# The indirect stores of routing records written through views of their table that are declared disjoint

## The chip, the cores and the metric

The kernel runs on one core of a Trainium2 chip. The metric is the device time of one execution in microseconds (us). TensorE (PE) does matmuls, VectorE (DVE) and ScalarE (ACT) do elementwise work, GpSimd (POOL) does reductions across partitions and issues indirect DMAs, SyncE (SP) issues the other DMAs. Each engine works through its own instructions in a fixed order and waits at an instruction until the semaphores that it names have come.

## The reference

Three layers follow one another on 2304 tokens of width 512. The third sends each token to one of eight experts; where a token's place in its expert's list is kept is what this change is about.

```python
# 1 attention: 4 batches x 8 heads, 576 tokens, head size 64, 128 random features
q_p, k_p = phi(q * scale), phi(k * scale)   # phi: exp(x @ omega.T - |x|^2/2 - max over features)
x = (q_p @ (k_p.T @ v)) / (q_p @ sum(k_p) + 1e-6)
# 2 dense layer, 512 -> 2048 -> 512
h = x @ w_in
x = (h * clip(h + 3, 0, 6) / 6) @ w_out
# 3 mixture of 8 experts, 512 -> 1024 -> 512; tokens with x @ w_skip <= 0 pass unchanged
e = argmax(x @ w_gate); g = softmax(x @ w_gate)[e]
out = x + g * (relu(x @ w1[e]) @ w2[e])
```

## The kernel before

The tokens go through the dense layer in six chunks of 512, 256, 384, 384, 384 and 384 (`CHS`), numbered 0 to 5. For each chunk sixteen steps run over the hidden width in pieces of 128. A step is a first product (L615, twelve matmuls: the operands are split into a high and a low part, and three products of the parts are summed; the last four use the low part `wil`, which SP loads again for every step into one of two buffers, L601), its activation on ACT and DVE (L621 to L636), and a second product into one bank of PSUM for each block of 128 tokens (L646).

Attention for batches 0 and 1 runs ahead of chunk 0 and within it; attention for batches 2 and 3 is spread among the steps of chunks 1 to 3. For a pair of heads (b, p) it projects queries on PE (L430), copies them on ACT to two tiles `pr` (L458), takes the maximum over the 128 features on POOL (`q_max`, a partition_all_reduce, L466), subtracts it on DVE (`q_sub`, L471), takes the exponential on ACT (`q_exp`, L475), and multiplies by the key sums on PE (`x_num`, L485, 40 small matmuls). The result is divided, transposed (L508) and written to `xh` and `xl`, the inputs of the dense layer.

When a chunk is done, its output is sent to DRAM (`x1d`), and the routing of its tokens follows: scores (`gate_dot`), the expert and the rank within it (`route_max` to `route_copy`), and the slot in the table (`route_slot`, L714 to L736). Then `route_put` (L738) stores, for each block of 128 tokens, 128 records of eight bytes (token number and weight) with an indirect DMA of POOL into the table `tab` in DRAM, at the slots. A chunk has as many stores as it has blocks: 4, 2, 3, 3, 3, 3, together 18. The slots of different tokens differ, but all 18 stores name the same rows of `tab` as their output, so the framework, which keeps the order of writes to overlapping regions, lets each store wait for the landing of the one before it.

The table is read in two places that this text speaks of. During chunk 5, SP loads 576 records of the fullest expert (`ga_rec`, L869) and 64 more of another (`s_rec`, `take_rec2`, L821); with these POOL gathers rows of `x1d` (L810) for the expert's matmuls, and at the end scatters the results to `out` (L815, L838). What is left goes through a loop at the end (L1482), whose body is not entered with these inputs.

The order on each engine comes from a list planner (`Schedule`): every operation is added with an engine, a cost, a due time and what it reads and writes, `plan` simulates them, and the instructions are emitted in that order. The planner knows the stores as POOL work of 1.04 us each, due at the chunk's routing time; it doesn't know of the waits between them, which the framework adds afterwards. DMAs that POOL issues signal their landing on one of eight counters, `DMASW0` to `DMASW7`, taken in turn.

Of the kernel before, what the change touches and what calls it, by code (L numbers as in the profile page):

```python
# [24 lines left out]
NT, DM, DFF = 2304, 512, 2048  # L25
# [4 lines left out]
C0 = [sum(CHS[:c]) for c in range(NCH + 1)]  # L30
# [11 lines left out]
TABN = NE * SEG  # L42
# [155 lines left out]
def performer_moe_kernel(  # L198
# [27 lines left out]


    tab = dram.tile([TABN + 128, 2], I32, name="tab")
    x1d = dram.tile([NT, DM], F32, name="x1d")
    wils = dram.tile([FT, 128, DM], F32, name="wils")  # L230

# [436 lines left out]
    rt = {}  # L668
# [68 lines left out]

    def route_put(c, t):  # L738
        G.indirect_dma_start(  # L739
            out=tab[0:TABN, :], out_offset=bass.IndirectOffsetOnAxis(ap=rt["slot"][:, t:t + 1], axis=0),  # L740
            in_=rt["rec"][:, t], in_offset=None, bounds_check=TABN - 1, oob_is_err=False)

    def begun(n8, name):
# [587 lines left out]
    def after(c):  # L1331
        t = START[c + 1]
        for k in range(TPC[c]):
            i = C0[c] // 128 + k
            sc.add("ACT", act(DM), t - 6, lambda k=k, i=i: x1_copy(i, accs[c, k]), r=[("acc", c, k), "x1p"], w=[("x1", i)],
                   t=[("ps", ("acc", c, k)), ("x1", i)])
            sc.add("SP", 2 * SPC, t + 1, lambda i=i: x1_out(i), r=[("x1", i)], o=[("wil", (c + 1, 3 + 2 * k))], w=[("x1d", c)], t=[("x1", i)],
                   nbytes=128 * DM * 8)
            for e in range(NE + 1):
                sc.add("DVE", 0.7, t + (AT["dot"] if c != CA - 1 else 0) + k * 9 if c < NCH - 1 else t + AT["dot5"] + k, lambda i=i, e=e: gate_dot(i, e), r=[("x1", i), "wg"], w=[("lg", c)],  # L1340
                       t=[("x1", i)])
        u = t + AT["route5"] if c == NCH - 1 else t + 25 if c == CA - 1 else t + AT["route"]
        sc.add("DVE", 0.3, u, lambda: route_max(c), r=[("lg", c), "rt"], w=[("rt0", c), "rt"])
        sc.add("ACT", 0.2, u, lambda: route_exp(c), r=[("rt0", c)], w=[("rt1", c)])
        sc.add("DVE", 0.9, u, lambda: route_hot(c), r=[("rt1", c)], w=[("rt2", c)])
        sc.add("PE", 0.1, u, lambda: route_rank(c), r=[("rt2", c)], w=[("rt3", c)], t=[("ps", ("rank", c))])
        sc.add("DVE", 0.2, u, lambda: route_copy(c), r=[("rt3", c)], w=[("rt5", c)], t=[("ps", ("rank", c))])
        sc.add("DVE", 3.1, u, lambda: route_slot(c), r=[("rt5", c), "cnt"], w=[("rt4", c), "cnt"])
        for k in range(TPC[c]):

            sc.add("POOL", 1.04, u, lambda k=k: route_put(c, k), r=[("rt4", c), "tab0"], w=["rt", ("tab", c)], nbytes=1024,
                   o=["ga_rec", "s_rec"] if c >= CA else [])
# [185 lines left out]
```

## Time and profile before

| | |
|---|---|
| time, median of 3 runs | 624.19 us (622.95 to 625.39) |
| the profiled execution: its own time | 624.3 us |
| its span in the trace | 622.4 us |
| mean granted clock of TensorE | 0.991 of full |
| PE busy | 599.8 us, 96% of the span |
| DVE busy | 440.7 us, 71% |
| ACT busy | 291.1 us, 47% |
| POOL busy | 110.3 us, 18% |

Times in the trace are in us from the start of the span. The execution's own time is 1.9 us longer than the span. The chain of waits that ended last holds only the last scatter and does not reach back into the kernel, so for this profile the waits of TensorE, which is busy nearly throughout, say more.

### The profile page before, as it was taken

The numbers are of one execution on the slowest core, as the hardware profiler recorded it, in microseconds if no ns is written. First come the engines' busy times: TensorE is split into PE (matmuls) and PEld (weight loads), VectorE is DVE, ScalarE is ACT, GpSimd is POOL, SyncE is SP. The second block draws the span as 40 slices with busy tenths as digits, with TensorE's granted clock in tenths as the row PEclk, the third lists the DMA queues.
The fourth block names the chain that finished last, engine by engine and source line by source line (L and its number), as shares of the span: only waits on it lengthen the run. The fifth ranks groups of instructions, "written<-read, shape, count | busy, mean of one in ns | idle before, by whom it ended". The sixth has DMA issues, their size and how long they took to land. (4 is left out here: it accounts for less than half of the span.)

```text
span 622.4 us, 11811 instructions
## 1 busy us (share of the span) xinstructions
PE 599.8 (96%) x4350; PEld 510.6 (82%) x4350; DVE 440.7 (71%) x1198; ACT 291.1 (47%) x672; POOL 110.3 (18%) x83
## 2 busy tenths in 40 slices
PE   9899999999999999999999999799999999999994
PEld 8677777788888898889988888799899889797883
DVE  3889999998769969863269673549722887449861
ACT  4776988677532456442234653332222323443220
POOL 2225034000020022221002043100010002402431
PEclk9999999999999999999999999899999999999998
DMA  7566466366366346322334313124212423892311
GB/s 281 163 196 189 151 202 212 117 217 203 99 231 185 99 141 176 90 67 56 68 91 148 108 65 52 34 85 136 68 52 68 135 89 99 265 351 69 92 45 53
DMA packets 38412, 81.66 MB, mean 131 GB/s; under 512 B 5740, under 2 KB 6380, under 8 KB 38352
## 3 DMA queue, kind: packets, MB, share of 16 engines
q1 hardware_dynamic: 36144, 76.90, 40.1%
q0 software_dynamic: 1776, 3.56, 1.9%
q8 instruction: 35, 0.57, 0.4%
q10 hardware_dynamic: 432, 0.43, 0.2%
q14 instruction: 25, 0.20, 0.1%
HBM read 65.88 MB, written 15.25 MB: 130 GB/s over the span
## 5 line engine op out<-in xcount | busy, mean ns | idle before, releaser
L646 PE MATMUL acc<-wo,gh 128*128 128x512 f32 x576 | 184.2, 401 | 0.2 <-ACT gh L630 0.2
L661 DVE CUSTOM_DVE_ANT_0 idle<-x,wg 128x512 uint8<-128x512 f32 x162 | 115.2, 711 | 7.6 <-ACT x L652 4.5
L646 PEld LDWEIGHTS acc<-wo,gh 128*128 128x128 f32 x576 | 103.9, 188 | 20.0 <-ACT gh L630 0.8
L621 ACT ACTIVATE g<-mm,half_t 128x384 f32<-128x384 f32 (+2 forms) x96 | 55.8, 581 | 126.6 <-PE mm L615 118.9
L646 PE MATMUL acc<-wo,gl 128*128 128x512 f32 x288 | 114.4, 397 | 0.1
L466 POOL PARTITION_ALL_REDUCE mx<-pr x32 | 67.6, 2160 | 234.1 <-ACT pr L458 227.7
L626 DVE SCALAR_TENSOR_TENSOR g<-g,mm 128x384 f32<-128x384 f32 (+2 forms) x96 | 52.8, 551 | 66.1 <-ACT g L621 65.6
L615 PE MATMUL mm<-xh,wih 128*128 128x384 f32 (+2 forms) x384 | 85.3, 344 | 0.1
L630 ACT CAST gh<-g 128x384 fp32r<-128x384 f32 (+2 forms) x96 | 49.3, 514 | 73.4 <-PE acc L646 46.6
L615 PE MATMUL mm<-xl,wih 128*128 128x384 f32 (+2 forms) x384 | 82.5, 336 | 0.0
L636 DVE TENSOR_TENSOR gl<-g,gh 128x384 fp32r<-128x384 f32 (+2 forms) x96 | 53.3, 556 | 33.4 <-ACT gh L630 33.2
L615 PEld LDWEIGHTS mm<-xh,wih 128*128 128x128 f32 x384 | 67.8, 189 | 9.0 <-DVE xl L520 0.2
L615 PEld LDWEIGHTS mm<-xl,wih 128*128 128x128 f32 x384 | 66.7, 188 | 2.8
L615 PE MATMUL mm<-xh,wil 128*128 128x384 f32 (+1 forms) x320 | 66.0, 328 | 1.0 <-DMA wil<-wils 1.0
L646 PEld LDWEIGHTS acc<-wo,gl 128*128 128x128 f32 x288 | 54.1, 188 | 13.8 <-DVE gl L636 0.9
L739 POOL DMA_INDIRECT tab<-rec,r_sloti x18 | 18.4, 1024 | 211.4 <-DVE rec L735 177.3
L615 PEld LDWEIGHTS mm<-xh,wil 128*128 128x128 f32 x320 | 54.6, 188 | 1.3 <-DMA wil<-wils 1.3
L393 ACT ACTIVATE kp<-att,kmx 128x128 f32<-128x128 f32 x160 | 45.5, 384 | 14.9 <-DVE kmx L378 14.8
L471 DVE TENSOR_TENSOR pr<-pr,mx 128x576 f32<-128x576 f32 x32 | 31.3, 978 | 8.4 <-POOL mx L466 8.4
L378 DVE TENSOR_REDUCE kmx<-att 128x2 f32<-128x256 f32 (+1 forms) x64 | 28.1, 482 | 8.2 <-PE att L372 5.1
L475 ACT ACTIVATE pr<-pr 128x576 f32<-128x576 f32 x32 | 22.1, 690 | 22.3 <-DVE pr L471 21.6
L485 PE MATMUL att<-kv,pr 128*64 128x65 f32 x640 | 25.1, 234 | 4.8 <-ACT pr L475 4.2
(204 smaller groups left out, 768.2 us busy)
## 6 DMA issues: line engine op xcount, KB each, us to landing
wil<-wils SPq DMA_DIRECT2D x80, 256.0 KB
w<-w_in SPq DMA_DIRECT2D x16, 512.0 KB
w<-w_out SPq DMA_DIRECT2D x16, 512.0 KB
vx<-vn SPq DMA_DIRECT2D x16, 322.5 KB
qr<-qt SPq DMA_DIRECT2D x16, 288.0 KB
out<-x SPq DMA_DIRECT2D x18, 256.0 KB
x1d<-x SPq DMA_DIRECT2D x18, 256.0 KB
kr<-kt SPq DMA_DIRECT2D x15, 288.0 KB
```

The costliest lines, as they stand in the source:

```text
L378: V.reduce_max(out=mx[:, 0:n], in_=st[key, b, p, g, h][:, 0:n * M].rearrange("p (g m) -> p g m", m=M), axis=AX.X, negate=True)
L393: A.activation(kp[:, i], ps[:, i * M:(i + 1) * M], AF.Exp, bias=mx[:, i:i + 1], scale=1.0)
L466: G.partition_all_reduce(mx, st["e", b, p, r], channels=128, reduce_op=bass_isa.ReduceOp.max)
L471: V.tensor_sub(pr, pr, st.pop(("qm", b, p, r)))
L485: T.matmul(ps[m:m + 64, i * 130 + r * 65:i * 130 + r * 65 + 65], st["e", b, p, r][:, s0 + m:s0 + m + 64], kv[:, r * 65:(r + 1) * 65], star ...
L615: T.matmul(ps[:, 0:CHS[c]], w[:, k, :], x[:, k, d], start=(n == 0), stop=(n == 3 * KC - 1))
L621: A.activation(t, mmp[c, f][:, 0:CHS[c]], AF.Relu, bias=half_t, scale=2.0 ** -UP / 6.0)
L626: V.scalar_tensor_tensor(out=t, in0=t, scalar=1.0, in1=mmp.pop((c, f))[:, 0:CHS[c]], op0=ALU.min, op1=ALU.mult)
L630: A.copy(gh, gt[c, f])
L636: V.tensor_sub(gl, t, gh.bitcast(F32))
L646: T.matmul(accs[c, t], g[:, ts], w[:, r, f % 2, :], start=(f == 0 and j == 0), stop=(f == FT - 1 and j == 2))
L661: V.tensor_tensor_reduce(out=idle.bitcast(mybir.dt.uint8), in0=x1[i], in1=wg[:, e, :], scale=1.0, scalar=0.0, op0=ALU.mult, op1=ALU.add, a ...
```

## The change

The table gets 18 views, one for each block of tokens, that the framework is told are disjoint, and each store writes through the view of its block. The reads of the table still name the table itself. The rest of the kernel is as it was; two more lines ahead of them move the numbers of all later lines by two.

```diff
--- before.py
+++ after.py
@@ -226,6 +226,8 @@
 
 
     tab = dram.tile([TABN + 128, 2], I32, name="tab")
+
+    tabs = dram_disjoint_views(tab, NT // 128)
     x1d = dram.tile([NT, DM], F32, name="x1d")
     wils = dram.tile([FT, 128, DM], F32, name="wils")
 
@@ -737,7 +739,7 @@
 
     def route_put(c, t):
         G.indirect_dma_start(
-            out=tab[0:TABN, :], out_offset=bass.IndirectOffsetOnAxis(ap=rt["slot"][:, t:t + 1], axis=0),
+            out=tabs[C0[c] // 128 + t][0:TABN, :], out_offset=bass.IndirectOffsetOnAxis(ap=rt["slot"][:, t:t + 1], axis=0),
             in_=rt["rec"][:, t], in_offset=None, bounds_check=TABN - 1, oob_is_err=False)
 
     def begun(n8, name):
```

No instruction changes its place on any engine: only the waits differ. On POOL, the place during chunk 3 at which the three stores of chunk 2 stand, with the last `q_max` pairs of attention around them (`mx` is the maximum, `rec` and `r_sloti` the records and slots) and the first store of chunk 3 behind; before:

```order
L466 ISA mx<-pr 128x576 [waits DVE_49,Activation_49] x4
L739 DMA tab<-rec,r_sloti 19456x2 [waits DMASW5_49,DVE_49]
L739 DMA tab<-rec,r_sloti 19456x2 [waits DMASW6_49,DVE_49]
L739 DMA tab<-rec,r_sloti 19456x2 [waits DMASW7_49,DVE_49]
L466 ISA mx<-pr 128x576 [waits Activation_49,Pool_49] x2
L739 DMA tab<-rec,r_sloti 19456x2 [waits DMASW0_49,DVE_49]
```

and with the change (`DMASW0` in the third store is the counter whose turn has come again, last used by the very first store of the kernel):

```order
L468 ISA mx<-pr 128x576 [waits DVE_49,Activation_49] x4
L741 DMA tab<-rec,r_sloti 19456x2 [waits DVE_49] x2
L741 DMA tab<-rec,r_sloti 19456x2 [waits DMASW0_49,DVE_49]
L468 ISA mx<-pr 128x576 [waits Activation_49,Pool_49] x2
L741 DMA tab<-rec,r_sloti 19456x2 [waits DMASW1_49,DVE_49]
```

The stores of one chunk no longer name the landing of the store before them, and the instructions behind them are the same. On SP, the place in chunk 5 where the records of the fullest expert are loaded; before:

```order
L870 TENSOR_LOAD ra [waits DVE_49]
L870 ISA x2
L873 ISA
L873 DMA ga_rec<-tab 128x2x2 [waits DMASW6_49]
L873 ISA
L873 DMA ga_rec<-tab 128x2x2
L874 ISA
L874 DMA ga_rec<-tab 64x2
```

and with the change:

```order
L872 TENSOR_LOAD ra [waits DVE_49]
L872 ISA x2
L875 ISA
L875 DMA ga_rec<-tab 128x2x2 [waits DMASW4_49,DMASW5_49,DMASW3_49,DMASW6_49,DMASW2_49,DMASW7_49,DMASW1_49,DMASW0_49]
L875 ISA
L875 DMA ga_rec<-tab 128x2x2
L876 ISA
L876 DMA ga_rec<-tab 64x2
```

The first load of the records, which before named only the counter of the last store, now names all eight counters; what stands behind it on SP is unmoved.

## Rows read from the trace of the kernel before

**Rows 1.** The page, part 1: busy time, share of the span and instructions of each engine

```profile
PE 599.8 (96%) x4350; PEld 510.6 (82%) x4350; DVE 440.7 (71%) x1198; ACT 291.1 (47%) x672; POOL 110.3 (18%) x83
```

**Rows 2.** Waits of TensorE, 210 to 622: who waited for whom, total, times, longest

```profile
PE att L485 <- ACT pr L475: 4.0, 2, 3.2
PE mm L615 <- DMA wil<-wils: 1.0, 1, 1.0
```

**Rows 3.** TensorE timeline, 370 to 402: start, duration, engine, line, operation [idle before <-releaser]

```profile
375.75 1.34 PE L485 MATMUL att<-kv,pr 128*64 128x65 f32 x40
376.91 0.64 PE L409 MATMUL att<-vx,kp 128*64 128x65 f32 x16
...
387.95 0.40 PE L646 MATMUL acc<-wo,gl 128*128 128x512 f32 x1
...
392.70 2.22 PE L485 MATMUL att<-kv,pr 128*64 128x65 f32 x36 [0.80 <-ACT pr L475]
394.85 1.36 PE L615 MATMUL mm<-xh,wih 128*128 128x384 f32 x4
396.05 0.88 PE L615 MATMUL mm<-xl,wih 128*128 128x384 f32 x4
396.76 0.87 PE L615 MATMUL mm<-xh,wil 128*128 128x384 f32 x4
```

**Rows 4.** Windows: stretch, length, busy (x instructions) PE PEld DVE ACT POOL, clock, DMA, GB/s

```profile
392.70:396.10 3.40, 3.40 (x41) 3.28 (x42) 2.21 (x8) 0.93 (x2) 0.00 (x0) 0.55 0.00 0
580.00:613.50 33.50, 33.50 (x188) 28.45 (x186) 21.22 (x79) 10.09 (x23) 13.19 (x14) 1.00 0.24 71
```

**Rows 5.** GpSimd timeline, 370 to 402

```profile
376.62 1.01 POOL L739 DMA_INDIRECT tab<-rec,r_sloti  x1 [5.66 <-DVE rec L735]
380.81 0.97 POOL L739 DMA_INDIRECT tab<-rec,r_sloti  x1 [3.18 <-DVE xl L520]
386.07 0.97 POOL L739 DMA_INDIRECT tab<-rec,r_sloti  x1 [4.28 <-DMA tab<-rec,r_sloti]
387.06 3.88 POOL L466 PARTITION_ALL_REDUCE mx<-pr  x2
```

**Rows 6.** VectorE timeline, 370 to 402

```profile
380.25 0.82 DVE L520 TENSOR_TENSOR xl<-att,xh 128x384 fp32r<-128x384 f32 x2 [0.97 <-ACT xh L516]
389.03 1.71 DVE L471 TENSOR_TENSOR pr<-pr,mx 128x576 f32<-128x576 f32 x1 [7.96 <-POOL mx L466]
```

**Rows 7.** ScalarE timeline, 370 to 402

```profile
378.32 1.34 ACT L458 COPY pr<-att 128x288 f32<-128x288 f32 x4
...
391.96 0.68 ACT L475 ACTIVATE pr<-pr 128x576 f32<-128x576 f32 x1
```

**Rows 8.** GpSimd timeline, 500 to 600

```profile
515.61 0.97 POOL L739 DMA_INDIRECT tab<-rec,r_sloti  x1 [58.54 <-DVE rec L735]
...
523.25 0.97 POOL L739 DMA_INDIRECT tab<-rec,r_sloti  x1 [3.80 <-DMA wraw<-w]
...
594.70 1.05 POOL L810 DMA_INDIRECT xgc<-x1d,ga_rec  x1 [0.27 <-POOL xgc L809]
```

**Rows 9.** SyncE waits, 500 to 560

```profile
SPq L873 <- DMA tab<-rec,r_sloti: 3.3, 1, 3.3
```

**Rows 10.** SyncE timeline, 515 to 540

```profile
529.79 0.53 SPq L601 DMA_DIRECT2D wil<-wils  x1
```

**Rows 11.** TensorE timeline, 525 to 536

```profile
531.99 0.86 PE L615 MATMUL mm<-xl,wih 128*128 128x384 f32 x4
533.88 0.97 PE L615 MATMUL mm<-xh,wil 128*128 128x384 f32 x4 [1.03 <-DMA wil<-wils]
```

**Rows 12.** One line's instructions, L739: durations in ns min/median/max, first and last start

```profile
L739 POOL DMA_INDIRECT tab<-rec,r_sloti x18: 967/974/1483, 220.2 to 592.9; - x18
L739 POOLq EVENT_SEMAPHORE  x17: 17/17/3092, 223.2 to 589.1; - x17
...
DMA to landing us min/median/max: 2.1/2.9/5.6
```

## The prediction

> **What bounds the kernel now.** I began with the busy shares on the page: TensorE (PE) is busy for 599.8 us, 96% of the span, and the next engine, VectorE (DVE), for 71% [rows 1]. The reader is to see that a gain elsewhere counts only where PE stands still for it or runs slower for it. So the second view was the waits of PE from 210 us on, since the first routing store comes at 220.2 [rows 12]. The rows shown are the only two of more than half a microsecond there: 4.0 us, in two pieces, for the exponentials of attention (`pr`, L475), and 1.0 us for a low weight part (`wil`) [rows 2]. Third, the timelines around these two places, followed backwards from engine to engine until something is found that the change touches. Both end at an indirect store of routing records, and the two are worked out below as places A and B. Last, the tail: from 580.00 to 613.50 PE is busy for 33.50 of 33.50 us at full clock [rows 4], so whatever PE gains before 580 arrives at the end, and nothing that merely comes earlier on another engine there does.
>
> **The change, part by part.** Nothing is added to any engine and nothing moves; a store takes POOL 967 to 1483 ns before and after [rows 12]. What goes is the wait of a store for the landing of the one before it, 2.1 to 5.6 us from issue to landing [rows 12]. A store in the change still waits for a counter that a DMA eight turns back used, which landed long ago, or for nothing but its records. Which of the 18 stores matter is decided by what is queued behind them on POOL.
>
> *Place A, the three stores of chunk 2.* They start at 376.62, 380.81 and 386.07, and at 387.06 the last pair of `q_max` follows without a gap [rows 5]. That the pair starts 0.02 us after the last store's instruction, over 2 us before that store can have landed, shows that POOL itself is free as soon as the instruction is over. The inputs of the pair, four copies of ACT, were ready at 378.32 + 1.34 = 379.66 [rows 7]. So the pair stood 7.4 us behind stores that were waiting for each other. DVE, done at 381.07, stood idle for 7.96 us until the first maximum came, and took it at 389.03 [rows 6]; the second exponential was over on ACT at 391.96 + 0.68 = 392.64 [rows 7], and PE went on with `x_num` at 392.70 [rows 3]. PE had finished its work ahead of that at 387.95 + 0.40 = 388.35 [rows 3].
>
> In the change the stores come one behind the other: 376.62 + 1.01 + 0.97 + 0.97 = 379.57 [rows 5]. The pair then starts at 379.7, when its inputs are there. From the start of the pair to the end of the last exponential it took 392.64 - 387.06 = 5.58 us, so that `x_num` could start at 385.3, three microseconds before PE comes to it. Were all three stores as long as the longest, 1.48 us, POOL would be free at 381.1 and `x_num` ready at 386.7, still ahead of PE. The wait therefore vanishes, with 1.7 to 3 us to spare.
>
> The price of the wait is more than its 4.0 us. After it, from 392.70 to 396.10, the granted clock was 0.55 [rows 4], so mostly the lower of the two levels, 1.2 GHz, where it was 2.4 GHz before. `x_num` undisturbed took 376.91 - 375.75 = 1.16 us for 40 matmuls, and four matmuls of the first product at full clock 396.76 - 396.05 = 0.71 us [rows 3]. So without the wait the second group of that step (L615, `xl`) starts at 388.35 + 1.16 + 0.71 = 390.22 instead of 396.05 [rows 3]: **5.8 us**, of which 4.0 are the waits, 3.35 - (0.9 x 1.16 + 0.71) = 1.6 the lower clock, and 0.2 the four matmuls between the two waits. The low end, if the clock fell for another reason, is 4.0. I take 5.8, since PE did nothing else unusual ahead of the fall.
>
> Here a rule speaks against the change. The rows say that a store took POOL at most 1.48 us, whatever DVE did beside it [rows 12]; the stores brought forward to 377.6 and 378.6 now stand beside a DVE that works until 381.07 [rows 6]. The Trainium skill (SBUF — State Buffer, section "SBUF: two separate sides") holds that GpSimd cannot write the descriptors of its own DMAs while DVE uses their shared port in a fast mode, and the next section of that page has a DMA of about 620 ns take about 3100 ns in this way. By that figure, an estimate, the two stores would hold POOL until 383.8 and `x_num` would be ready at 389.4, one microsecond late, which would leave 618.2 us. The traces so far don't bear it out: in none of the 18 stores does the instruction reach half of that.
>
> *Place B, the three stores of chunk 4.* They start at 515.61 and, waiting for each other, up to 523.25 [rows 8]; the last had landed at about 523.25 + 2.1 = 525.35, and SP stood for 3.3 us until then at the load of the expert's records (`ga_rec`) [rows 9]. Queued behind it on SP are the other loads of records and the load of the next `wil`, which went out at 529.79 [rows 10]. PE needed it one group after 531.99, so at 531.99 + 0.71 = 532.70, and got it at 533.88 [rows 11]: **1.2 us**. In the change the third store starts at 515.61 + 2 x 0.97 = 517.55. SP's wait ends with the landing of the last of the three: with the median landing, 2.9 us [rows 12], at 520.5, before SP comes to it (525.35 - 3.3 = 522.05); with the longest, 5.6, at 523.2. SP so gains 2.2 to 3.3 us, more than the 1.2 that are needed. That SP now names eight counters instead of one costs seven semaphore instructions that are already satisfied; on POOL such a one takes 17 ns [rows 12], so some 0.1 us, inside that reserve. The gathers of `x1d` and their transposes, which wait for the same records, come earlier by the same amount, so they don't take the place of the wait.
>
> *The other twelve stores.* Behind those of chunks 0, 1 and 3 POOL has nothing whose input is ready, and no wait of PE in [rows 2] leads there: nothing. Behind those of chunk 5 stands the last gather at 594.70 [rows 8], which feeds only the last weighing of results, after the last matmuls, and PE is busy without a gap until 613.50 [rows 4]: nothing as long as PE sets the end, and should PE shrink there too, the gather comes earlier with the stores.
>
> *Sum.* 624.3 us of the profiled execution - 5.8 - 1.2 = 617.3. It lies 0.1 above the median of the runs, 624.19, so I write 617.2.
>
> **The rivals.**
> - *Only A pays.* Three stores in flight at once could land later than one by one, and then SP waits as before. Condition: a landing after 522.05 + (3.3 - 1.2) = 524.15, so 6.6 us after the third store's start, where 5.6 was the longest seen. For it: three at once have not been seen here on this table. Time: 624.2 - 5.8 = 618.4.
> - *A new wait at A.* Between the pair of maxima and `x_num` ACT and DVE have pieces of the dense layer's steps to do, which lay in the pause before; if one of them, waiting for PE in its turn, now stands ahead of an exponential, half of the gain may go: 624.2 - 2.9 - 1.2 = 620.1. Against it: a reserve of 1.7 to 3 us.
> - *Nothing changes.* POOL could be held by the store in flight, inside the instruction rather than ahead of it, as the descriptors of the next store have to wait for room. Then every store is as late as before: 624.2. Against it: POOL began other work 0.02 us after a store [rows 5], though not another store.
> - *Slower.* One mechanism at B: if the small writes of stores in flight hinder each other on the way to DRAM, the last lands late, SP stands at the records with `wil` behind it, and PE stands for `wil`. PE goes on 533.88 - 525.35 = 8.5 us after the landing. Compared with before, PE loses what the landing loses against 525.35, so the gain of A is used up if the last store lands after 525.35 + 5.8 = 531.2, that is 13.6 us after its start. Three times the longest landing, 16.8 us, would give 534.35: 624.2 - 5.8 + 9.0 = 627.4. For it speaks only that landings differ by more than a factor of two already one by one; against it, that 13.6 is 2.4 times the longest.
>
> **How the numbers follow.** Forecast 0.74; only A 0.10; a new wait at A 0.05; nothing 0.07; slower 0.04. The forecast's own range is that of the runs of before, 1.2 either way: 616.0 to 618.4. To hold 8 in 10 it must take in the case in which only A pays, with its own spread, and part of the next: 615.6 to 620.4. A change of under 0.5%, 3.1 us, can't be told from none. Faster by more (below 621.1): the first three cases, 0.89, of which I give 0.01 to their spread, 0.88. Within: 0.08. Slower: 0.04.
>
> **What would show it.** Right at A: three stores on POOL within about 3 us of the first, the `q_max` pair some 7 us earlier in relation to them, DVE's idle time of 8 us ahead of `q_sub` gone, no wait of PE at L485, and the granted clock at full behind it. Right at B: the load of `ga_rec` without a wait of 3 us on SP, and no wait of PE for `wil`. In all else the busy times stay, and the tail after 580 is the same, some 7 us earlier. Wrong would be: gaps of 2 us and more between stores of one chunk as before, store instructions of 2 us and more, or a later landing that SP waits for.

## The result: 615.1 us, and the profile after

The change takes 615.07 us (median of 6 runs, 614.49 to 615.74); the kernel before took 623.25 us (6 runs, 622.25 to 625.39; three of them are those of the first table, and the three others have the median 622.72). The ratio is 0.987, with an interval of 0.9853 to 0.9888: faster by 1.1 to 1.5%. The forecast was 617.2 with a range of 615.6 to 620.4, so the time lies 0.5 us below the range. The profiled execution of the change has a span of 612.6 us, against 622.4.

Both predicted waits are gone. The page of the change, part 1, against [rows 1], and then the waits of TensorE from 210 to 622 (who waited for whom, total, times, longest), against [rows 2]:

```profile
PE 595.7 (97%) x4350; PEld 507.4 (83%) x4350; DVE 440.7 (72%) x1198; ACT 291.2 (48%) x672; POOL 110.7 (18%) x83
```

```profile
PE att L374 <- DVE g L628: 0.2, 1, 0.2
```

The same instructions run, PE is busy 4.1 us less for the same 4350 matmuls, and the two rows on L485 and on `wil` are missing. What is left is a fifth of a microsecond.

Place A. GpSimd's timeline (start, duration, engine, line, operation [idle before <-releaser]), which answers to [rows 5]:

```profile
373.92 1.01 POOL L741 DMA_INDIRECT tab<-rec,r_sloti  x1 [5.65 <-DVE rec L737]
375.24 0.97 POOL L741 DMA_INDIRECT tab<-rec,r_sloti  x1 [0.30 <-issue]
376.51 0.97 POOL L741 DMA_INDIRECT tab<-rec,r_sloti  x1 [0.30 <-issue]
377.51 3.88 POOL L468 PARTITION_ALL_REDUCE mx<-pr  x2
```

The three stores follow each other at 1.3 us, where they took 4.2 and 5.3 us before, and the pair of maxima begins 3.59 us after the first store instead of 10.44. VectorE's, ScalarE's and TensorE's timelines answer to [rows 6], [rows 7] and [rows 3]:

```profile
379.48 1.71 DVE L473 TENSOR_TENSOR pr<-pr,mx 128x576 f32<-128x576 f32 x1 [1.33 <-POOL mx L468]
```

```profile
382.41 0.69 ACT L477 ACTIVATE pr<-pr 128x576 f32<-128x576 f32 x1
```

```profile
385.24 0.40 PE L648 MATMUL acc<-wo,gl 128*128 128x512 f32 x1
385.56 1.39 PE L487 MATMUL att<-kv,pr 128*64 128x65 f32 x40
386.88 0.96 PE L617 MATMUL mm<-xh,wih 128*128 128x384 f32 x4
387.68 0.86 PE L617 MATMUL mm<-xl,wih 128*128 128x384 f32 x4
```

The second exponential is over at 383.10, 2.5 us before PE comes to `x_num`, and the row of `x_num` has no wait. The granted clock behind it, from the windows (columns as in [rows 4], whose first row it answers to), is full:

```profile
385.50:389.00 3.50, 3.50 (x53) 3.37 (x53) 2.26 (x9) 0.45 (x1) 0.00 (x0) 1.00 0.02 8
```

From the first store of chunk 2 to the group `xl` behind `x_num` it was 396.05 - 376.62 = 19.43 us, and is 387.68 - 373.92 = 13.76: place A gave 5.67 us, where 5.8 were forecast.

Place B. The timelines of GpSimd, SyncE and TensorE, which answer to [rows 8], [rows 9, 10] and [rows 11]:

```profile
507.18 0.97 POOL L741 DMA_INDIRECT tab<-rec,r_sloti  x1 [64.12 <-DVE rec L737]
508.46 0.97 POOL L741 DMA_INDIRECT tab<-rec,r_sloti  x1 [0.30 <-DVE a_oh L1127]
509.74 1.08 POOL L741 DMA_INDIRECT tab<-rec,r_sloti  x1 [0.30 <-DVE used L1133]
```

```profile
513.90 0.97 SPq L875 DMA_DIRECT2D ga_rec<-tab  x2
...
518.32 0.53 SPq L603 DMA_DIRECT2D wil<-wils  x1
```

```profile
523.57 0.86 PE L617 MATMUL mm<-xl,wih 128*128 128x384 f32 x4
524.27 0.87 PE L617 MATMUL mm<-xh,wil 128*128 128x384 f32 x4
```

SP's load of the records no longer waits, `wil` goes out 11.14 us after the first store of the chunk instead of 14.18, and the matmul on it comes at once, 17.09 us after that store instead of 18.27: place B gave 1.18, where 1.2 were forecast. One store still costs what it did, and lands as it did, against [rows 12] (durations in ns min/median/max, first and last start):

```profile
L741 POOL DMA_INDIRECT tab<-rec,r_sloti x18: 971/977/1484, 217.5 to 579.2; - x18
...
DMA to landing us min/median/max: 2.1/3.0/5.0
```

The two spans differ by 9.8 us, though, and A and B together by 6.85. Of the rest 2.70 us lie ahead of the first store of chunk 2, and, with 220.17 us against 217.47 for the very first store, in a part of the program in which the change touches nothing. The windows of the head tell the executions apart; from 28 to 36 us, first before, then the change:

```profile
28.00:36.00 8.00, 7.79 (x106) 6.55 (x104) 5.68 (x16) 5.96 (x18) 0.86 (x1) 0.79 0.61 209
```

```profile
28.00:36.00 8.00, 7.79 (x107) 6.57 (x105) 6.84 (x19) 6.79 (x20) 2.46 (x2) 1.00 0.89 283
```

The execution of before had a stretch of lower clock there, that of the change had one from 20 to 24 us, and others have none in the head. Both kernels have executions with either kind of head, as the table below shows, and this pair of profiles so overstates the change.

### The profile page after: what moved, and what is told of

The parts are those of the page before. It is cut to its first block, busy times and chain, and to the rows that moved or that the text cites. A ratio compares the mean times of both kernels' runs of the same rounds, so it can differ in the third digit from the quotient of the medians.

```text
span 612.6 us, 11813 instructions
## 1 busy us (share of the span) xinstructions
PE 595.7 (97%) x4350; PEld 507.4 (83%) x4350; DVE 440.7 (72%) x1198; ACT 291.2 (48%) x672; POOL 110.7 (18%) x83
## 5 line engine op out<-in xcount | busy, mean ns | idle before, releaser
L374 PE MATMUL att<-wb,kr 64*128 64x128 f32 x320 | 26.5, 292 | 1.3 <-DVE xl L522 0.8
```

Source lines behind the costliest of these rows:

```text
L374: T.matmul(st[key, b, p, g, h][:, i * M:(i + 1) * M], x[half(h), min(c * 128, S - 128):min(c * 128 + 128, S)], wb[half(h), :], start=True, ...
```

## The experiments

Twelve runs followed, on three further chips, four to a chip, each time beside the kernel before. "A" and "B" are the places of the prediction. The time at each is read from GpSimd's timeline, from the first store of chunk 0 to that of chunk 3 (place A lies between) and from there to that of chunk 5 (place B). Where no wait of PE is left between, they are 222.0 and 136.6 us in every trace, within 0.05, so what stands above these is what the place costs in that execution (in the row "the wait filled", A holds the added matmuls too):

| kernel, as traced | first store of chunk 0 | of 3 | of 5 | 0 to 3 | 3 to 5 | A | B |
|---|---|---|---|---|---|---|---|
| before | 220.17 | 447.91 | 585.83 | 227.74 | 137.92 | 5.7 | 1.3 |
| views unused | 218.41 | 446.24 | 583.81 | 227.83 | 137.57 | 5.8 | 1.0 |
| views for chunk 2 | 217.91 | 444.30 | 582.28 | 226.39 | 137.98 | 4.4 | 1.4 |
| views for chunk 4 | 218.54 | 446.41 | 583.00 | 227.87 | 136.59 | 5.9 | 0.0 |
| views for the others | 220.02 | 449.98 | 589.18 | 229.96 | 139.20 | 8.0 | 2.6 |
| the wait filled | 218.21 | 445.96 | 586.89 | 227.75 | 140.93 | 5.8 | 4.3 |
| third store waits | 218.44 | 441.99 | 578.62 | 223.55 | 136.63 | 1.6 | 0.0 |
| maxima first, no views | 220.04 | 442.08 | 579.71 | 222.04 | 137.63 | 0.0 | 1.0 |
| the change, first chip | 217.47 | 439.50 | 576.10 | 222.03 | 136.60 | 0.0 | 0.0 |
| the change, second chip | 218.32 | 444.62 | 581.22 | 226.30 | 136.60 | 4.3 | 0.0 |
| the change, third chip | 218.78 | 445.29 | 581.93 | 226.51 | 136.64 | 4.5 | 0.0 |
| the change, fourth chip | 220.17 | 442.17 | 578.77 | 222.00 | 136.60 | 0.0 | 0.0 |
| change and maxima first, third chip | 217.63 | 439.58 | 576.21 | 221.95 | 136.63 | 0.0 | 0.0 |
| change and maxima first, fourth chip | 218.01 | 440.01 | 576.62 | 222.00 | 136.61 | 0.0 | 0.0 |

### The second chip: parts of the change, and the change again

Before on this chip: 622.58 us.

**Views declared, and not used.**

```diff
     tab = dram.tile([TABN + 128, 2], I32, name="tab")
+
+    tabs = dram_disjoint_views(tab, NT // 128)
```

> The views are declared and no store uses them: the instructions and their waits are those of the kernel before. Theory T (places A and B are all that the change does, 5.7 + 1.3 us; what the medians differ by beyond that, 8.2 - 7.0 = 1.2 us, is the spread of executions in the first 60 us): 0.0 us against before, within 0.5. Rival H (the change also does something to the start of the program): if the declaration alone did it, -1.2 us.

Measured: 622.87 us, ratio 0.9998 (0.9983 to 1.0014). PE waits 4.0 us at L487, as in [rows 2]. The declaration alone does nothing that shows.

**Views for the stores of chunk 2 alone.** The declaration is as above; the diffs of this and the next partial versions show the store alone, with the rest of its line left out (`...`).

```diff
-            out=tab[0:TABN, :], ...
+            out=(tabs[C0[c] // 128 + t] if c in (2,) else tab)[0:TABN, :], ...
```

> Only the three stores of chunk 2 use the views; the other fifteen name the table as before and wait for one another. Theory T: place A alone, -5.7 us (617.5 where before has 623.2), PE's wait of 4.0 us at the exponentials gone, its wait of 1.0 us for wil still there. Rival H: A and B together are larger than their traces show, so -6.5 to -6.9. Rival, B causes part of A: less than -5.

Measured: 621.96 us, ratio 0.9982 (0.9966 to 0.9997). That is 0.6 us less than before, where 5.7 were expected: a miss, far below the 5.8 us of place A, though its wait is gone. By its number alone this is the rival "B causes part of A" of the expectation; TensorE's waits show that something else stands in the place of A:

```profile
PE att L432 <- ACT kv L417: 2.4, 1, 2.4
PE mm L617 <- DMA wil<-wils: 1.1, 1, 1.1
```

A new wait of 2.4 us at `q_proj` (L432), for a copy of ScalarE. I call it the hold, and come back to it.

**Views for the stores of chunk 4 alone.** The diff is that of chunk 2 with `c in (4,)`.

> Only the three stores of chunk 4 use the views. Theory T: place B alone, -1.3 us, PE's wait for wil gone, its 4.0 us at the exponentials still there with the low clock behind. Rival H: -2 or more.

Measured: 621.36 us, ratio 0.9975 (0.9959 to 0.9992), 1.2 us less than before. PE's wait for `wil` is gone and the 4.0 us at L487 stand. Place B alone has its forecast worth.

**The change again.**

> The change itself once more, beside before on the same chip. Theory T: -7.0 us, so that the 8.2 us of the first medians shrink; of that 5.7 at A and 1.3 at B. Rival H: -8.2 again.

Measured: 619.49 us, ratio 0.9936 (0.9914 to 0.9958), so only 3.1 us less than before; on the first chip it was 8.2. Both theories of the expectation (7.0 and 8.2) were missed. The trace has the hold. TensorE's timeline, its windows and ScalarE's timeline of this run:

```profile
375.02 0.64 PE L411 MATMUL att<-vx,kp 128*64 128x65 f32 x16
375.58 1.39 PE L432 MATMUL att<-qr,wb 64*128 64x288 f32 x6
379.35 0.75 PE L432 MATMUL att<-qr,wb 64*128 64x288 f32 x2 [2.38 <-ACT kv L417]
```

```profile
381.00:384.40 3.40, 3.40 (x12) 3.40 (x12) 2.53 (x3) 0.33 (x3) 3.29 (x2) 0.50 0.02 5
```

```profile
375.19 0.51 ACT L632 CAST gh<-g 128x384 fp32r<-128x384 f32 x1 [1.40 <-DVE g L628]
379.03 0.27 ACT L417 COPY kv<-att 128x130 f32<-128x130 f32 x1 [3.33 <-remote]
```

The copy of `kv` needs only the product `k_kv` (L411), whose last matmul was over at 375.66, and ScalarE was free at 375.70. It starts at 379.03. PE comes to `q_proj`, wants the buffer that this copy empties, and stands for 2.38 us; then the clock falls to 0.50, 1.2 GHz, for 3.4 us. That is 2.4 + 1.7, and some 0.2 that is left over, the 4.3 us in the table: most of what place A had given is lost again, 12 us earlier in the same stage.

The semaphore records of the same trace tell what the copy waited for. PE's own end signal, which rises with each finished group, came with gaps (us from the span's start):

```
change, second chip: 377.472  379.009  379.052  379.094  379.137
change, fourth chip: 377.090  377.556  378.226  378.268  378.858
```

In the upper row nothing is signalled for 1.54 us, and then four ends come 43 ns apart, although the matmuls that they belong to were over by 376.97 at the latest. In the lower row, from the run on the fourth chip below, they come as the matmuls end. So by the trace PE had finished, and its signals were late. As the ends of matmuls are modelled in the profile, this does not tell where between the last matmul's start and the signal the time went.

### The third chip: what the hold hangs on

Before on this chip: 623.78 us. Two theories. Either the hold comes from the stores issued close behind each other beside the many short matmuls of `x_num`, `k_kv` and `q_proj` (then stores that come later, or further apart, have less of it), or it belongs to this place of the program or to the chip (then it stays wherever the stores are).

**The change, a third time.**

> The change once more. Its second measurement came out 3.1 us faster than before, its first 8.2: in the second profile the end signals of the matmuls at 375 (end of x_num, k_kv, q_proj) reach ScalarE and VectorE up to 3.4 us late while the three stores are being issued, and TensorE waits 2.4 us at L432 with the low clock behind. Theory S (the stores, issued close together beside this stretch, hold these signals back, on some chips or placements): either 615 (no hold) or 619.5 (hold), by the profile. Rival P (the hold has nothing to do with the stores, it belongs to the place and the chip): the same two values, and it stays when the stores are moved.

Measured: 619.81 us, ratio 0.9935 (0.9911 to 0.9959). The hold is there, 2.5 us at L432.

**The third store of chunk 2 through the table, the rest as in the change.**

```diff
+            out=(tabs[C0[c] // 128 + t] if (c, t) != (2, 2) else tab)[0:TABN, :], ...
```

> The change, but the third store of chunk 2 names the table itself, so it waits for the landing of the other two. Theory T: q_max starts some 4 us later than in the change and is still in time, so no wait at L487 or under 1 us. Theory S: with only two stores close together the hold, where it comes, ends earlier, about 0.7 us after the second store's end instead of the third's; PE's wait at L432 about 1 us shorter than in e10, total 1 to 2 us below e10. Without the hold: equal to e10 within 0.5. Rival P: equal to e10 in either case.

Measured: 617.18 us, ratio 0.9901 (0.9877 to 0.9925): faster than the change on the same chip, by 2.6 us, with one store more that waits. TensorE's waits, a window behind the wait, and GpSimd's timeline:

```profile
PE att L432 <- ACT kv L417: 1.1, 1, 1.1
```

```profile
380.00:382.00 2.00, 2.00 (x13) 1.95 (x12) 0.82 (x2) 0.36 (x2) 1.29 (x2) 1.00 0.07 8
```

```profile
374.93 1.01 POOL L741 DMA_INDIRECT tab<-rec,r_sloti  x1 [5.66 <-DVE rec L737]
376.24 0.97 POOL L741 DMA_INDIRECT tab<-rec,r_sloti  x1 [0.31 <-issue]
380.69 0.97 POOL L741 DMA_INDIRECT tab<-rec,r_sloti  x1 [3.47 <-DVE xl L522]
381.69 3.88 POOL L468 PARTITION_ALL_REDUCE mx<-pr  x2
```

With two stores in a row instead of three the copy of `kv` started at 377.92, so 0.7 us after the second store's end at 377.21. With three it started at 379.03 and 379.69 on the second and third chip, 0.75 and 0.87 after the third's end. The hold lasts as long as the row of stores. The gain is more than the 1 to 2 us that were expected: the wait is 1.4 us shorter, where about 1 was forecast, and this wait of 1.1 us is followed by no low clock, which is worth another 1.7.

**The kernel before with the last maxima of attention ahead of chunk 2's stores.** No views; GpSimd's order alone is changed.

```diff
-                   o=["ga_rec", "s_rec"] if c >= CA else [])
+                   o=["ga_rec", "s_rec"] if c >= CA else [("qm", r, 3, 3) for r in range(2)] if c == 2 else [])
```

> The kernel before, without views, with the three stores of chunk 2 put behind the last q_max pair on GpSimd; they still wait for one another. Theory T on place A (what costs is what stands behind the stores on GpSimd): PE's wait of 4.0 us at L485 gone, -5.7 us, so 617 where before has 622.6, and place B unchanged with its 1.0. Theory S: no late signals at 375, since the stores come later. Rival P: a hold of 2 to 4 us appears here as well, -1 to -2 us.

Measured: 618.23 us, ratio 0.99 (0.9874 to 0.9926), 5.5 us less than before. The stores still wait for each other, at 383.40, 387.82 and 392.46, and of PE's waits only that for `wil` is above 0.2 us:

```profile
PE mm L615 <- DMA wil<-wils: 0.7, 1, 0.7
```

So what place A cost was exactly that the maxima stood behind the stores; how long the stores themselves take matters to nobody there.

**Both: the change, and the maxima first.** The two diffs together.

> The change, with the stores of chunk 2 put behind the last q_max pair. Theories T and S: -7.0 us whatever the chip, 615.5, no late signals at 375, no wait of PE over 0.5 us from 210 on. Rival P: as e10 where that has the hold (619.5).

Measured: 615.62 us, ratio 0.9869 (0.9846 to 0.9892), 4.2 us less than the change on the same chip. GpSimd's timeline and TensorE's waits:

```profile
376.82 3.91 POOL L468 PARTITION_ALL_REDUCE mx<-pr  x2 [8.43 <-ACT pr L460]
380.90 0.99 POOL L741 DMA_INDIRECT tab<-rec,r_sloti  x1 [0.17 <-issue]
382.20 1.06 POOL L741 DMA_INDIRECT tab<-rec,r_sloti  x1 [0.30 <-issue]
383.56 0.97 POOL L741 DMA_INDIRECT tab<-rec,r_sloti  x1 [0.30 <-issue]
```

```profile
PE att L374 <- DVE g L628: 0.2, 1, 0.2
```

The same three stores in as close a row, some 7 us later beside the dense layer's matmuls, hold nothing back. The theory that the place of the program or the chip alone makes the hold is refuted: on one chip it is there with the stores at 375 and gone with the stores at 381. PE signals far less often there (at 381.27, 383.62 and 385.49 in this trace, each within 0.03 us of a matmul's end), so the runs do not tell whether it is the short matmuls or the many signals that the stores must stand beside.

### The fourth chip: the remaining stores, the clock, and both versions once more

Before on this chip: 624.32 us (23 runs).

**Views for all chunks but 2 and 4.** The diff is that of chunk 2 with `c in (0, 1, 3, 5)`.

> Views for the stores of chunks 0, 1, 3 and 5 alone; chunks 2 and 4 keep the table. The prediction's theory puts nothing at these twelve stores: within 1 us of the kernel before, with the wait of 4.0 us at the x_num matmul of the last pair still there, and the second wait of 1.0 us at wil. A theory that every store's wait costs a little, 8.2 us over 18 stores, gives 12 of 18 of it, 5.5 us less than before. A gain over 1.5 us would refute the first.

Measured: 623.43 us, ratio 0.9992 (0.9972 to 1.0012). The other twelve stores are worth nothing, as forecast. But its traced execution, at 627.64 us the slowest of its twelve, shows places A and B, whose stores wait as in the kernel before, in another execution. TensorE's waits and two windows behind A, against [rows 2] and the first row of [rows 4]:

```profile
PE att L487 <- ACT pr L477: 5.2, 2, 4.5
PE mm L617 <- DMA wil<-wils: 1.0, 1, 1.0
PE acc L648 <- ACT gh L632: 0.8, 1, 0.8
```

```profile
392.60:396.00 3.40, 2.68 (x41) 2.37 (x41) 2.05 (x5) 2.08 (x5) 0.00 (x0) 0.50 0.00 0
396.00:398.80 2.80, 2.80 (x11) 2.80 (x10) 1.62 (x8) 0.00 (x0) 0.00 (x0) 0.50 0.00 0
```

The wait is 5.2 us instead of 4.0, since the stores took longer to land: the third could start 10.67 us after the first (376.50 to 387.17), in [rows 5] after 9.45. And the low clock lasts on through the second window, in which in [rows 3] four matmuls took 0.87 us again, as at full clock. Place A cost 8.0 us here, and 5.7 in the execution from which I predicted. Place B cost 2.6 instead of 1.3: the wait for `wil` was followed 4.3 us later by another, of 0.76, in the dense layer.

**The wait of place A filled with matmuls.**

```diff
+        if (b, p, g) == (3, 3, 0):
+            for _ in range(26):
+                T.matmul(ps[:, 0:128], ident, ident, start=True, stop=True)
```

> The kernel before with 26 matmuls of 128 columns on the identity put ahead of the x_num matmul that waits 4.0 us in the last pair; their result is overwritten. They leave the wait of the data as it is and fill most of it with work on TensorE. If the half clock of 3.41 us behind the wait comes from the idle 4.0 us, the row behind it shows the full clock and the kernel is about 1.6 us faster than before although it computes more; if the low clock has another cause, the time is that of before or up to 1 us longer.

Measured: 623.35 us, ratio 0.9981 (0.9966 to 0.9996): 1.0 us less than before, with more to compute. TensorE's timeline (which has two records for each added matmul) and windows:

```profile
386.13 5.97 PE L483 MATMUL att<-ident 128*128 128x128 f32 x52
392.02 1.39 PE L488 MATMUL att<-kv,pr 128*64 128x65 f32 x40
```

```profile
392.02:396.00 3.98, 3.98 (x58) 3.88 (x58) 2.27 (x9) 0.27 (x1) 0.00 (x0) 1.00 0.02 4
...
534.00:537.60 3.60, 3.60 (x11) 2.85 (x10) 1.95 (x4) 2.40 (x5) 0.00 (x0) 0.54 0.82 257
```

The filling was longer than the wait: the last exponential was over at 390.63, and `x_num` starts at 392.02. Behind it the clock is full. So the low clock of place A does come from the idle time ahead of it, as the prediction took it. A gain at A this trace does not show: the surplus of 1.4 us takes back nearly all of the 1.6, and with the filling A stands at 5.8 in the table, as in the trace of before. The measured 1.0 us (by the interval of the ratio 0.2 to 2.1) would fit executions of before in which A costs more, as in the run above, but no trace shows it. The last window is at place B of the same run. There PE waited 2.6 us for `wil`, not 1.0, and this wait was followed by low clock too; the place cost 4.3 us.

**The change, a fourth time.**

> The change once more, beside a new run of the kernel before. Theory of the hold (the three stores of chunk 2, issued back to back beside x_num, k_kv and q_proj of the last pair, hold back the end signals of TensorE): where the trace shows the kv copy of ScalarE 3 us late and TensorE waiting 2.4 us at q_proj, the gain is 3 to 4.5 us; where it shows neither, the gain is 7 to 8.5 us. A trace with the wait and 8 us of gain, or without it and 3 us, would refute it.

Measured: 615.84 us, ratio 0.9861 (0.9831 to 0.9891), 8.5 us less than before. No hold: ScalarE's copy of `kv` follows the work ahead of it without a gap, and `q_proj` does not wait, though the first store stands 0.87 us behind the start of the `x_num` ahead of it, as on the second and third chip.

```profile
376.60 1.01 POOL L741 DMA_INDIRECT tab<-rec,r_sloti  x1 [5.66 <-DVE rec L737]
377.91 0.97 POOL L741 DMA_INDIRECT tab<-rec,r_sloti  x1 [0.30 <-issue]
379.19 0.97 POOL L741 DMA_INDIRECT tab<-rec,r_sloti  x1 [0.31 <-issue]
```

```profile
377.58 0.27 ACT L417 COPY kv<-att 128x130 f32<-128x130 f32 x1
```

**The change with the maxima first, once more.**

> The views, and the last pair's q_max ahead of the stores of chunk 2 on GpSimd, once more beside the change. Theory of the hold: the stores start some 4 us later, beside other matmuls, no wait at q_proj, 7 to 8.5 us less than before whether or not the change beside it shows the hold. If it is the chip that decides and not the place of the stores, it gains as much as the change beside it, within 1 us.

Measured: 616.16 us, ratio 0.9872 (0.9845 to 0.9899), the same as the change beside it. Both alternatives of the expectation agree with that, as there was no hold to avoid on this chip. Of the two versions this is the safer one: 8.2 us less than before on both chips on which it ran, where the change gave 4.0 and 8.5.

## Why the prediction missed

- **What bounds the kernel, and where the change acts:** right. Two places and no other: the views of chunk 2 and chunk 4 remove the waits, the twelve other stores give 0.9992 (0.9972 to 1.0012).
- **Place A:** the chain from the stores over the maxima to `x_num` was right, and changing the order of the maxima alone gives 5.5 us without any view. The size was right in the traced pair, 5.67 against 5.8, and so was the reserve, 2.5 us against "1.7 to 3". The cause of the low clock was right (the filled wait).
- **Place B:** right, 1.18 and 1.2 against 1.2. The stores did not land later with three at once (at most 5.0 us against 5.6), so neither "only A pays" nor the slower rival had a ground.
- **The rule on GpSimd's descriptors** that spoke against the change: the second and third store took 0.97 us each in all four traces of the change; in the first, VectorE was busy for 0.90 of the second one's 0.97 us. The wait of GpSimd that the Trainium skill (SBUF — State Buffer, section "SBUF: two separate sides") describes for a VectorE in a fast mode did not occur at these stores. Whether VectorE was in such a mode beside them the traces do not tell, so the rule itself is not tested.
- **The step that failed is the sum**, and in it the number from which it starts: "624.3 us of the profiled execution". The mechanism at A and B was right; the part of the program that the change does not touch was taken from one execution, and that was not the usual one. It differed in two ways that stood against each other, so that its time lay beside the median all the same.
  - *Its head was long.* The first store came at 220.17 us. In the 14 traces of the table it comes at 217.5 to 218.8 in ten, and at 220.0 to 220.2 in four; these four are the traces with lower clock at 30 to 33 us. One of them is among the eight traces with chunk 2's views, three among the six others: both kinds of kernel have both heads, nothing in the change reaches that far back, and so few traces show no dependence. From there on the change takes 222.0 + 136.6 + 36.6 us, and 1.9 lie around the span: with a head of 220.17 that makes 617.3, which is the forecast. The change's execution with such a head, traced on the fourth chip, did take 617.26. The measured median, 615.07, stands for a head of 218.0. The 2.1 us by which the forecast was too high are this.
  - *A and B were cheap in it*, at least against the fourth chip. I took 5.8 and 1.2 for prices of the kernel, and on the second chip the traces bear them out (A 5.8 and 5.9, B 1.0). In the traces A cost 5.7 to 8.0 where chunk 2's stores waited ahead of the maxima, and B 1.0 to 4.3. The "1.6 the lower clock" is about twice that when the low clock lasts on, the "4.0 of the waits" are 5.2 when stores land late, and the wait for `wil`, for which I counted no low clock, has it when it is 2.6 us long. In the change both are nought wherever there is no hold. The medians so differ by 8.2 and 8.5 us (first and fourth chip), and not by 7.0; of the first the interval of the ratio allows 7.0 to 9.2, and against the three newer runs of before alone it is 7.7. So on the first chip this point is not shown.
- What supports the second point beyond two traces is the mean granted clock of whole executions. On the fourth chip 23 executions of before had 0.986 to 0.994 (median 0.990), the four of the change 0.994 to 0.997. In the traces a stretch of 3.4 us at half clock is worth about 0.003 of that mean: 0.996 with none but the one at the kernel's end (change and maxima first, third chip), 0.991 with two more (before), 0.988 with three more (views for the others). The one at the end, in these traces 3.7 to 6.6 us of the span, moves the mean by another 0.002 from execution to execution. By that the change saves about two such stretches there, give or take one, where I counted one. How often the untraced executions have them at A, at B or in the head is not shown.
- **The range** was too narrow for it: its lower end, 615.6, is the forecast less 1.2, the spread of three runs of before, and less 0.4 more, and has nothing for a head shorter by 2 us.
- **The rival "a new wait at A"** had the chance 0.05 and the wrong middle: I looked for it between the maxima and `x_num`, where there is none, and not at the stores themselves. On two of the four chips there is a new wait, 2.4 us at `q_proj` with the clock behind it; it gives back 4.3 to 4.5 us and leaves 619.5 to 619.8, near that rival's 620.1. The forecast had nothing of it, and on these chips it would have been too low by more than 2 us.

What stays open: why the same program with its stores at the same point has the hold on the second and third chip and not on the first and fourth, and how stores on GpSimd's queue delay TensorE's end signals. The runs show that the hold goes with the row of stores, in length and in place. They do not show the way. Chip by chip the traces agree: on the second and third every one with stores of chunk 2 at this point has the hold (on the second for a shorter time also with a single store), and on the fourth none of three has it. The trace of before, with a single store there, has it for 0.6 us, that of the change on the first chip has not; whether these two ran on one chip is not on record.

## What to carry to other kernels

Ask of each waiting instruction who is queued behind it on its engine: here the waits of eighteen stores cost nothing, but for the two chunks behind which other engines' work was standing, and putting that work first gave as much as removing the wait. A sum that starts from one profiled execution inherits its luck, in stretches that the change never touches too: look in the clock's slices for low stretches, and give the range their worth in both directions. And work that no longer waits runs beside something else than before, so look at what it now stands beside, not only at what it released.

## What the runs showed of the hardware

- Three indirect stores of 128 records issued 1.3 us apart on GpSimd, beside the short matmuls of attention, held back TensorE's end signals on two chips: a ScalarE copy that needed only such a signal started 3.3 to 3.5 us late, 0.7 to 0.9 us after the last store's instruction was over. Beside the dense layer's matmuls the same stores held back nothing.
- A single store at that point did it for a shorter time: with chunk 2 through the table the same copy was 0.5 to 0.6 us late, in the trace of before (its line below) and in two on the second chip; in the two on the fourth chip it was not late.

```profile
378.15 0.27 ACT L415 COPY kv<-att 128x130 f32<-128x130 f32 x1 [0.56 <-PE att L409]
```

- An idle wait of TensorE of 4.0 us was followed by 3.4 us at 1.2 GHz in one execution and one of 5.2 us by over 6 us in another; of the waits for `wil`, that of 1.0 us was followed by none and that of 2.6 us by 3.4 us; of the waits at `q_proj`, that of 1.1 us by none and that of 2.4 us by 3.4 us.
